# First chunk's blocks solved on VectorE and feed-forward groups of two chunks, in place of feed-forward groups of three chunks

## The chip, the cores and the metric

The kernel runs on one core of a Trainium2 chip. The core has five engines with queues of their own, each working through its instructions in order: TensorE (PE in the profile; its weight loads are shown apart as PEld), VectorE (DVE), ScalarE (ACT), GpSimd (POOL) and SyncE (SP, which only issues DMAs here). Engines wait for one another through semaphores. TensorE writes its results to PSUM, which DVE and ACT read; everything else is in SBUF, and the inputs, the output and some intermediate arrays are in HBM.

The metric is the device time of one execution in microseconds: 1093.16 us, the median of three runs (1090.8, 1093.16 and 1096.74). A difference of about 0.5% is the least that a measurement of this kernel can tell from none.

## What is computed

Two stages. The first is a recurrence over 768 positions for 4 batches of 8 heads, with a 40 x 40 state each; the second is a feed-forward layer with a squared ReLU over the 3072 tokens that come out. The weights of the second stage arrive as 64-bit floats, everything else as 32-bit floats.

```python
# r, k, v, w, a, b: (4, 8, 768, 40)
for t in range(S):
    y[:, :, t] = einsum('bhd,bhde->bhe', rt, state)
    Sa = einsum('bhde,bhe->bhd', state, at)
    state_decay = state * wt[:, :, None, :] - einsum('bhd,bhe->bhde', Sa, bt)
    state = state_decay + einsum('bhd,bhe->bhde', vt, kt)
x = y.transpose(0, 2, 1, 3).reshape(B * S, H * D)      # 3072 x 320
h = maximum(x @ w_in, 0.0)                              # 320 x 2048
out = h * h @ w_out                                     # 2048 x 320
```

## The kernel before

**Tiling.** The 768 positions are cut into chunks of 128. One unit of work is a chunk of one batch with all its 8 heads; there are 24, numbered so that chunk 0 to 3 are the first chunk of each batch, 4 to 7 the second, and so on. Only chunks of the same batch depend on each other through the state.

**Work of one chunk.** `early(i)` turns w, a and b with TensorE (line 316), multiplies the decays up along time (scans, lines 353 and 354; reciprocals, 357 and 358; products with b and a, 361 and 362), forms a matrix N of the chunk on TensorE, and stores N and the decays in HBM (`kept_q`, `kept_m`, `kept_n`, `kept_d`, `kept_e`). `solve(u)` inverts the triangular diagonal blocks of N: a loop of 31 or 63 steps, each of one multiplication (line 432, result in `half_p`) and one subtraction (line 434, in `half_t`), all on POOL. For the first chunks the blocks are 32 x 32 (31 steps), later 64 x 64. `take(u)` fetches a unit's blocks (`half_n`) before, and the result is stored to `kept_t`. `inverses(i)` fetches it as `blocks`, and puts the 64 x 64 inverse T together with a transposition on DVE (line 466) and small matmuls. `rest(i)` loads k, r, v and b of a chunk, turns them, and makes the masked products A and RV. `chain(i)` is the part that must go in the order of the chunks: x from A and the state, T, N, T again, a transposition, the new state (line 595), RX, and the chunk's output `tokens` (line 614).

**Feed-forward.** The generator `ffn()` takes the output of a group of `GB = 3` chunks at once: 384 columns. For each of 16 blocks of 128 hidden units it multiplies by `w_third` (64 rows: the remainder of the 320 input rows, two blocks side by side on the two halves of the array) and by `w_in` (two times 128 rows), then ACT applies ReLU (line 641) and DVE multiplies by the value before it, which squares it (line 642). Each 32-bit matmul shows as two in the profile. Two blocks make a pair, whose results lie in two PSUM buffers of the pool `ps_f`, which has two; the last group uses the pool `ps_w` with four. Then for each chunk of the group 16 matmuls by `w_out` (320 columns) are summed up. The generator yields after each block and after each quarter of a chunk's second part, so a group is 16 + 12 = 28 steps. Before a group can start, its `tokens` rows are moved to where the matmuls want them: eight small DMAs on SP.

**Weights.** Since they are 64-bit, `rounding()` makes 32-bit floats of them piece by piece with ACT and DVE (lines 258 to 277), 26 pieces in all, of which the first 10 are needed before feed-forward can start. The raw words are fetched into memory that is free at that time: `w_out` and the later `hid`.

**Order of the work.** It is written out by hand. A prologue calls the generators of chunks 0 to 3 step by step with `go`, with `solve(0)`, `solve(1)` and `solve(2)` in between. Then the loop over the 24 chunks interleaves ("weaves"), in 12 steps per chunk: `chain(i)`, `rest(i + 1)`, `early` of chunks further on, 10 steps of `ffn()` and some pieces of `rounding()`. In chunks 0 to 3 no feed-forward step runs, in chunk 4 there are 8 (from its step 4 on). What is left of `ffn()` runs after the loop. Each engine follows the order in which this program emits its instructions; a wait at the head of a queue stops all behind it. Loads and stores go through SP's queue in the order of emission, `take` and the store after `solve` through POOL's.

**Rings.** Inputs have ring buffers: two each for k, b and v, one for r.

Of the kernel before, what the change touches and what calls it, by code (L numbers as in the profile page):

```python
# [11 lines left out]
Alu = mybir.AluOpType  # L12
# [5 lines left out]
def kernel(  # L18
# [22 lines left out]
    nc = tc.nc  # L41
# [8 lines left out]
    NP = H // 2  # L50
    DP = 64
    NF = DFF // 128
    GB = 3

# [34 lines left out]
    def single(name, shape):  # L89
        return const.tile(shape, FP32, tag=name, name=name)  # L90
# [40 lines left out]

    def more_rings():
        for nm in ("k", "b", "r", "v"):
            rings[nm] = Ring(f"in_{nm}", 1 if nm == "r" else 2, [128, H, DP], 0.0, pads)

    order = [(bb, c) for c in range(NCH) for bb in range(B)]
    loaded, early_loaded = {}, {}
# [45 lines left out]

    UP, DOWN, A_ = range(3)
    decays = Ring("decay", 2, [128, 3, NP, C + 2], 1.0, whole)
    minus_x = Ring("minus_x", 1, [128, H, DP], 0.0, pads)
    states = Ring("state", B, [128, NP, 2, DP], 0.0, whole)

    w_in = single("w_in", [128, NT, DFF])
# [9 lines left out]


    room = w_out.rearrange("p f c -> p (f c)")
    hidden = single("hid", [128, NF, GB * C])
    free_words = hidden.rearrange("p f t -> p (f t)")
    lowest = single("lowest", [128, 1])
    nc.vector.memset(lowest, -896.0 * (1 << 23))
    wide = [room[:, 4 * WI * i:4 * WI * (i + 1)] for i in range(2)] + [free_words[:, :4 * WI]]

    in_turn = [free_words[:, at:at + 2 * DM] for at in [4 * WI + 2 * DM * i for i in range(4)] + [2 * DM * i for i in range(3)]]
    LENT = len(in_turn)


    runs = []
# [18 lines left out]
              [w_third[:, WI * i:WI * (i + 1)] for i in range(2)])  # L231
    NARROW = len(pieces)
    WIDE = len(fetches)
    for f in range(NF):
        fetchable(in_turn[f % LENT], [(0, 128, moe_w_out[f * 128:(f + 1) * 128, :])], [w_out[:, f, :]])

    then = {1: (3,), 2: (WIDE,), 3: (4,), 4: (WIDE + 1,), 5: (WIDE + 2,), 6: (WIDE + 3,), 7: (WIDE + 4,), 8: (WIDE + 5,),
            9: (WIDE + 6,)}
    then.update({NARROW + f: (WIDE + f + LENT,) for f in range(NF - LENT)})
    finished = [0]  # L240
    left = lambda: len(pieces) - finished[0]

# [93 lines left out]
    turned = lambda nm, bufs: new(nm, [128, NP, 128], bufs)  # L336


    def spare(name, i):
        at = NF * GB * C - (("mv", "turned", "joins").index(name) * 2 + i % 2 + 1) * H * Q  # L340
        return free_words[:, at:at + H * Q].rearrange("p (h t) -> p h t", h=H)

    def early(i, g=None):

# [63 lines left out]
        for col in range(cols):  # L408
            queues[col % len(queues)].dma_start(out=part_of(u)[col * rows:(col + 1) * rows], in_=kept)  # L409

    def solve(u, between={}):

        first, nb = units[u]
        fine = u < FINE
        size = Q if fine else HC
        cols = classes(u)
        rows = 128 // cols
        part = part_of(u)
        words = size // cols * size
        at = u * Q * Q // 2 if fine else 0  # L420
        ts = solved[:, at:at + words]
        nc.gpsimd.memset(ts, 0.0)
        for col in range(cols):
            nc.gpsimd.memset(ts[col * rows:(col + 1) * rows, col::size + cols], -1.0)
        t3 = ts.rearrange("p (j t) -> p j t", t=size)
        for s in range(size - 1):
            if s in between:
                between[s]()
            n, m_ = s // cols + 1, size - 1 - s
            at = s * size + s + 1 if s < Q else Q * HC + (s - Q) * (Q + 1) + 1  # L430
            p_ = new("half_p", [128, 528], 1)[:, :n * m_].rearrange("p (j t) -> p j t", j=n)
            nc.gpsimd.tensor_tensor(p_, part[:, at:at + m_].unsqueeze(1).to_broadcast([128, n, m_]),  # L432
                                    t3[:, :n, s:s + 1].to_broadcast([128, n, m_]), Alu.mult)
            nc.gpsimd.tensor_tensor(t3[:, :n, s + 1:], t3[:, :n, s + 1:], p_, Alu.subtract)  # L434
        to = kept_t[u]
        to = to.rearrange("n b h f k j t -> (n b h f k) (j t)") if fine else to.rearrange("n b h f j t -> (n b h f) (j t)")
        nc.gpsimd.dma_start(out=to, in_=ts)

# [52 lines left out]
    def rest(i, g):  # L491
# [14 lines left out]
        if soon(i):  # L506
            next(joining, None)
        yield
        g["A"] = masked("A", 2, kT, aT)
        yield  # L510
        while "v" not in x_:
            line.pop(0)[1]()
# [113 lines left out]
    def ffn():  # L626
        for gi in range(len(order) // GB):
            while gi not in gathered or finished[0] < NARROW:
                yield False
            t_ = tokens.pop(gi)  # L630
            hid = []
            for f in range(0, NF, 2):
                ps = [psum(ps_f if gi < len(order) // GB - 1 else ps_w)[:, :GB * C] for _ in range(2)]
                for e, p_ in enumerate(ps):
                    half = slice(e * DP, (e + 1) * DP)
                    mm(p_, w_third[half, f * 64:f * 64 + 128], t_[half, NT, :], True)
                for e, p_ in enumerate(ps):
                    for j in range(NT):
                        mm(p_, w_in[:, j, (f + e) * 128:(f + e + 1) * 128], t_[:, j, :], False)
                    h_ = hidden[:, f + e]  # L640
                    nc.scalar.activation(h_, p_, Act.Relu)  # L641
                    nc.vector.tensor_tensor(h_, p_, h_, Alu.mult)  # L642
                    hid.append(h_)
                    yield True
            while left():
                yield False
            for n in range(GB):
                bb, c = order[gi * GB + n]
                p_ = psum(ps_f if gi < len(order) // GB - 1 else ps_w)[:, :DM]
                for f in range(NF):  # L650
                    mm(p_, hid[f][:, n * C:(n + 1) * C], w_out[:, f], f == 0)
                    if f % PART == PART - 1 and f < NF - 1:
                        yield True
                o_ = new("o", [128, DM], 2)
# [6 lines left out]

    second = ffn()
    gathered = set()

    def run(gen):
        for _ in gen:
# [87 lines left out]
    tc.no_sync_barrier()  # L754


    TOTAL = 12
    ahead = {0: (4, 5), 1: (6, 7), 2: (8,), 3: (9,), 4: (10, 11), 5: (12, 13)}
    ahead.update({i: (i + 8,) for i in range(6, len(order) - 8)})
    share = {**{i: (0, 0) for i in range(B)}, B: (8, 4)}  # L760
    pieces_in = {0: (4, TOTAL), 1: (6, TOTAL), 2: (6, TOTAL), 3: (7, TOTAL), B: (4, 4)}
    done = set(range(B))
    unit = unit_of[B]
    for i in range(len(order)):
        bb, c = order[i]
# [10 lines left out]
        for j, m_ in enumerate(made):  # L776
            jobs.append((prepare(m_), 5, j * 5, TOTAL - 5 * (len(made) - 1 - j)))
        done.update(made)
        jobs.append((some(second, n), n, begin, TOTAL))
        if i in pieces_in:  # L780
            m_, end = pieces_in[i]
            jobs.append((some(rounded, 2 * m_), 2 * m_, 0, end))
# [38 lines left out]
```

## Time and profile before

| | before |
|---|---|
| median of three runs | 1093.16 us |
| profiled execution, whole time | 1096.74 us |
| profiled execution, span from first to last instruction | 1095.0 us |
| mean granted TensorE clock | 0.905 |
| HBM read and written | 75.77 and 34.48 MB |
| chunk outputs (line 614): first five | 92.8, 142.5, 189.3, 228.7, 274.4 us |
| chunk outputs: last | 1025.3 us |
| first feed-forward matmul | 244.8 us |
| POOL's last instruction in the table of stages | before 900 us |

The profile is of one execution. Its busy times count an engine's own instructions; the span is what they are shares of. Times in the timeline are counted from the span's start. The page's picture of the span in 40 slices shows TensorE at nine tenths or more from the eleventh slice (274 us) on, with a break in the last slices but two, and the granted clock between 0.5 and 0.8 of full speed in the first nine.

### The profile page before, as it was taken

What the parts mean: (1) busy time and instruction counts of PE and PEld (TensorE: products, weight loads), DVE (VectorE), ACT (ScalarE), POOL (GpSimd) and SP (SyncE); (2) the same over time, 40 slices, a digit from 0 to 9 for tenths busy, and PEclk for the clock granted to TensorE, in tenths of its full rate; (3) what the DMA queues carried; (4) which work ended last, traced back from release to release, by engine and by line L of the source; (5) the groups of instructions that cost most, each with busy time, mean ns of one, the idle gap of its engine ahead of it and who ended that gap; (6) DMA issues with size and microseconds to landing.
All of it is one profiled execution on the core that took longest, in us unless ns stands there. A gap on an engine that the chain in (4) does not pass through costs nothing.

```text
span 1095.0 us, 18413 instructions
## 1 busy us (share of the span) xinstructions
PE 996.7 (91%) x7248; PEld 746.5 (68%) x7248; DVE 470.3 (43%) x940; ACT 236.1 (22%) x483; POOL 653.2 (60%) x1127
## 2 busy tenths in 40 slices
PE   6286667889999999999999999999999999999798
PEld 5275566776677766777677667766786777667556
DVE  6458666686453265243452463252323322331030
ACT  2133222332221222113211222113112211230020
POOL 5787636885885999923999904999858820000000
PEclk8656655568999999899999999999999999999899
DMA  9879987767819524348616528414244331330000
GB/s 113 156 145 182 182 217 152 154 123 150 146 62 206 119 75 68 100 116 159 132 40 111 119 83 161 116 46 80 54 115 92 68 85 32 73 62 7 22 1 18
DMA packets 261350, 113.42 MB, mean 104 GB/s; under 512 B 243792, under 2 KB 249424, under 8 KB 259600
## 3 DMA queue, kind: packets, MB, share of 16 engines
q1 hardware_dynamic: 256928, 93.24, 43.3%
q0 software_dynamic: 3248, 18.88, 7.2%
q8 instruction: 57, 0.93, 0.4%
q10 hardware_dynamic: 1088, 0.13, 0.1%
q14 instruction: 29, 0.24, 0.1%
HBM read 75.77 MB, written 34.48 MB: 101 GB/s over the span
## 4 chain that ended last, share of the span: by engine, by line
PE 75%; DVE 9%; DMA 8%; POOL 3%; SPq 2%; issue 2%; ACT 1%; DVEq 0%; POOLq 0%; ACTq 0%
PE ps_f L87 35%; PE ps_c L87 19%; PE ps_w L87 13%; PE ps_w L316 4%; PE ps_w L532 1%; DMA half_n<-kept_d 1%; POOL half_p L432 1%; DMA dec<-kept_e 1%; DMA blocks<-kept_t 1%; POOL half_t L434 1%; SPq L108 1%; DVE decay L357 1%; DVE decay L358 1%; PE ps_c L542 1%; PE ps_c L585 1%
## 5 line engine op out<-in xcount | busy, mean ns | idle before, releaser
L432 POOL TENSOR_TENSOR half_p<-half_n,half_t 128x70 f32<-128x70 f32 (+52 forms) x502 | 289.4, 576 | 102.4 <-DMA half_n<-kept_d 53.8
L434 POOL TENSOR_TENSOR half_t<-half_t,half_p 128x70 f32<-128x70 f32 (+52 forms) x502 | 316.1, 630 | 39.3
L87 PE MATMUL ps_f<-w_out,hid 128*128 128x320 f32 x672 | 199.5, 442 | 0.0
L87 PE MATMUL ps_f<-tokens,w_in 128*128 128x384 f32 x448 | 174.6, 514 | 0.0
L642 DVE TENSOR_TENSOR hid<-ps_f,hid 128x384 f32<-128x384 f32 x112 | 61.8, 552 | 232.2 <-ACT hid L641 232.1
L87 PEld LDWEIGHTS ps_f<-w_out,hid 128*128 128x128 f32 x672 | 122.6, 192 | 44.4 <-issue 1.4
L87 PEld LDWEIGHTS ps_f<-tokens,w_in 128*128 128x128 f32 x448 | 78.0, 193 | 63.9 <-issue 33.2
L641 ACT ACTIVATE hid<-ps_f 128x384 f32<-128x384 f32 x112 | 55.0, 491 | 217.4 <-PE ps_f L87 217.4
L87 PEld LDWEIGHTS ps_c<-xr,T 64*64 64x64 f32 x768 | 55.4, 151 | 25.7 <-issue 22.1
L87 PE MATMUL ps_f<-tokens,w_third 64*128 64x384 f32 x224 | 62.2, 536 | 2.4 <-DVE w_out L266 1.3
L87 PE MATMUL ps_c<-xr,T 64*64 64x40 f32 x768 | 61.3, 242 | 3.3 <-ACT xr L566 1.0
L87 PEld LDWEIGHTS ps_c<-in_v,A 128*128 128x128 f32 x384 | 50.3, 206 | 4.1
L332 DVE TENSOR_TENSOR A<-ps_w,upper 128x512 f32<-128x512 f32 x48 | 30.9, 685 | 48.3 <-PE ps_w L87 48.3
L87 PE MATMUL ps_c<-in_v,A 128*128 128x40 f32 x384 | 49.6, 292 | 0.0
L332 DVE TENSOR_TENSOR RX<-ps_w,upper 128x512 f32<-128x512 f32 x48 | 30.8, 684 | 39.9 <-PE ps_w L87 39.8
L409 POOL DMA_DIRECT2D half_n<-kept_d x18 | 9.0, 504 | 64.7 <-DMA kept_d<-N 64.4
L353 DVE TENSOR_TENSOR_SCAN decay<-ps_w,ones 128x64 f32<-128x64 f32 x88 | 23.7, 270 | 51.2 <-PE ps_w L316 51.2
L87 PE MATMUL ps_w<-decay,bT 40*128 40x128 f32 x352 | 28.5, 308 | 17.9 <-DVE decay L362 15.6
L503 DVE TENSOR_TENSOR kvT<-ps_w,dec 128x512 f32<-128x512 f32 x24 | 16.4, 683 | 61.3 <-PE ps_w L316 36.6
L87 PE MATMUL ps_w<-rT,xnT 40*128 40x128 f32 x384 | 33.3, 302 | 9.7 <-DVE RV L332 8.6
L614 DVE TENSOR_TENSOR tokens<-ps_c,dec 128x512 f32<-128x512 f32 x24 | 16.5, 689 | 59.3 <-PE ps_c L87 59.3
L87 PEld LDWEIGHTS ps_w<-rT,xnT 40*128 40x128 f32 x384 | 27.8, 202 | 19.9 <-DVE RV L332 14.0
(138 smaller groups left out, 1456.6 us busy)
## 6 DMA issues: line engine op xcount, KB each, us to landing
kept_e<-decay SPq DMA_DIRECT2D x22, 780.0 KB
dec<-kept_e SPq DMA_DIRECT2D x22, 780.0 KB
hid<-in_moe_w_out_dram SPq DMA_DIRECT2D x16, 320.0 KB
half_n<-kept_d POOLq DMA_DIRECT2D x12, 384.0 KB, 10.2
half_n<-kept_d POOLq DMA_DIRECT2D x6, 768.0 KB, 11.0
in_w<-in_w_dram SPq DMA_DIRECT2D x24, 160.0 KB
in_ab<-in_b_dram SPq DMA_DIRECT2D x24, 160.0 KB
in_ab<-in_a_dram SPq DMA_DIRECT2D x24, 160.0 KB
```

Source lines behind the costliest of these rows:

```text
L87: nc.tensor.matmul(o, l_, r_, start=start, stop=True, skip_group_check=True)
L108: later(lambda: queue.dma_start(out=out_, in_=in_), steps)
L316: nc.tensor.transpose(p_[:, q * 128:(q + 1) * 128], pair(x_, q), ident)
L332: nc.vector.tensor_tensor(t_, p_, over4(upper), Alu.mult)
L353: nc.vector.tensor_tensor_scan(up[:, q, MID + 1:C + 1], wT[:, q, MID:], ones, 1.0, Alu.mult, Alu.mult)
L357: nc.vector.reciprocal(down[:, :, MID + 1:C + 1], up[:, :, MID + 1:C + 1])
L432: nc.gpsimd.tensor_tensor(p_, part[:, at:at + m_].unsqueeze(1).to_broadcast([128, n, m_]), t3[:, :n, s:s + 1].to_broadcast([128, n, m_]), ...
L434: nc.gpsimd.tensor_tensor(t3[:, :n, s + 1:], t3[:, :n, s + 1:], p_, Alu.subtract)
L503: nc.vector.tensor_tensor(kT, kT_, down[:, :, 1:C + 1], Alu.mult)
L614: nc.vector.tensor_tensor(t_, y_, g["up"][:, :, :C], Alu.mult)
L641: nc.scalar.activation(h_, p_, Act.Relu)
L642: nc.vector.tensor_tensor(h_, p_, h_, Alu.mult)
```

## The change

The feed-forward part works on groups of two chunks (256 columns) instead of three (384). With `GB = 2` there are 12 groups, a group has 16 + 8 = 24 steps, and 12 steps of it run in each chunk from chunk 4 on; in chunk 4, 8 more are emitted ahead of the chunk's other work. The hidden units get a 17th slot, and their slots go round. All weight pieces are made in chunks 0 to 3. With the memory that becomes free, two raw buffers of their own take weights, and the rings of r and of `minus_x` get a second buffer, A four buffers instead of two; the output buffer `o` has one instead of two.

In the prologue the first chunk's blocks are solved on DVE, with the intermediate product in PSUM, and stored and fetched through ACT's queue. Chunk 0's A, r and v steps and the loads of chunk 1 and of the third early chunk are emitted ahead of it, the decays of chunks 2 and 3 after it; the fetch of chunk 1's blocks follows it in the program but is on POOL's queue, which `solve(0)` no longer uses.

```diff
-    GB = 3
+    GB = 2
...
-            rings[nm] = Ring(f"in_{nm}", 1 if nm == "r" else 2, [128, H, DP], 0.0, pads)
+            rings[nm] = Ring(f"in_{nm}", 2, [128, H, DP], 0.0, pads)
...
-    minus_x = Ring("minus_x", 1, [128, H, DP], 0.0, pads)
+    minus_x = Ring("minus_x", 2, [128, H, DP], 0.0, pads)
...
-    hidden = single("hid", [128, NF, GB * C])
+    hidden = single("hid", [128, NF + 1, GB * C])
...
+    lent = [free_words[:, 2 * DM * i:2 * DM * (i + 1)] for i in range(3)]
+    own_ = [single(f"raw{i}", [128, 2 * DM]) for i in range(2)]
...
-    def solve(u, between={}):
+    def solve(u, between={}, engine=nc.gpsimd):
...
-            p_ = new("half_p", [128, 528], 1)[:, :n * m_].rearrange("p (j t) -> p j t", j=n)
-            nc.gpsimd.tensor_tensor(p_, part[:, at:at + m_].unsqueeze(1).to_broadcast([128, n, m_]),
+            p_ = new("half_p", [128, 528], 1) if engine is nc.gpsimd else psum(ps_f)
+            p_ = p_[:, :n * m_].rearrange("p (j t) -> p j t", j=n)
+            engine.tensor_tensor(p_, part[:, at:at + m_].unsqueeze(1).to_broadcast([128, n, m_]),
                                     t3[:, :n, s:s + 1].to_broadcast([128, n, m_]), Alu.mult)
-            nc.gpsimd.tensor_tensor(t3[:, :n, s + 1:], t3[:, :n, s + 1:], p_, Alu.subtract)
+            engine.tensor_tensor(t3[:, :n, s + 1:], t3[:, :n, s + 1:], p_, Alu.subtract)
...
-        nc.gpsimd.dma_start(out=to, in_=ts)
+        (nc.gpsimd if engine is nc.gpsimd else nc.scalar).dma_start(out=to, in_=ts)
...
-        g["A"] = masked("A", 2, kT, aT)
+        g["A"] = masked("A", 4, kT, aT)
...
-                    h_ = hidden[:, f + e]
+                    h_ = hidden[:, (gi * NF + f + e) % (NF + 1)]
...
-                o_ = new("o", [128, DM], 2)
+                o_ = new("o", [128, DM], 1)
...
+    STEPS = NF + 4 * GB
...
-    solve(0, {12: lambda: take(1, own)})
+    go(r0, 2)
+    load_early(3)
+    load(1)
+    flush()
+    solve(0, engine=nc.vector)
+    join = inverses(0, ready[0], nc.scalar)
+    go(join)
+    take(1, own)
     go(r0)
-    load_early(3)
-    go(r0, 4)
-    go(e2, 2)
-    load(1)
+    go(e2)
+    go(r0, 2)
     go(first_slot)
-    go(e2, 2)
-    go(e3, 2)
+    go(e2)
+    go(join)
+    go(e2)
+    go(e3)
+    go(join)
+    go(e2)
+    go(e3)
+    go(join)
...
-    join = inverses(0, ready[0])
-    go(join)
...
-    solve(1, {8: lambda: weights_by(0, nc.gpsimd), 20: lambda: take(2, own)})
+    solve(1, {14: lambda: weights_by(0, nc.gpsimd)})
+    take(2, own)
...
-    TOTAL = 12
+    TOTAL = STEPS // GB
...
-    share = {**{i: (0, 0) for i in range(B)}, B: (8, 4)}
-    pieces_in = {0: (4, TOTAL), 1: (6, TOTAL), 2: (6, TOTAL), 3: (7, TOTAL), B: (4, 4)}
+    share = {**{i: (0, 0) for i in range(B)}, B: (TOTAL, 8)}
+    pieces_in = {0: 4, 1: 7, 2: 8, 3: 8}
...
-        n, begin = share.get(i, (10, 0))
+        n, before = share.get(i, (TOTAL, 0))
+        for _ in range(before):
+            next(second)
+            tick()
...
-        jobs.append((some(second, n), n, begin, TOTAL))
+        jobs.append((some(second, n), n, 0, TOTAL))
```

More of the change, by code (lines that the diff above doesn't have):

```diff
@@ L206 @@
     wide = [room[:, 4 * WI * i:4 * WI * (i + 1)] for i in range(2)] + [free_words[:, :4 * WI]]
-    in_turn = [free_words[:, at:at + 2 * DM] for at in [4 * WI + 2 * DM * i for i in range(4)] + [2 * DM * i for i in range(3)]]
-    LENT = len(in_turn)
+    lent = [free_words[:, 2 * DM * i:2 * DM * (i + 1)] for i in range(3)]
+    own_ = [single(f"raw{i}", [128, 2 * DM]) for i in range(2)]
     runs = []
@@ L233 @@
     WIDE = len(fetches)
+    in_turn = [*own_, *lent]
     for f in range(NF):
[L235 to L239, printed above, removed]
+        fetchable(in_turn[f % 5], [(0, 128, moe_w_out[f * 128:(f + 1) * 128, :])], [w_out[:, f, :]])
+    then = {0: (WIDE,), 1: (3,), 2: (WIDE + 1,), 3: (4,), 5: (WIDE + 2, WIDE + 3), 6: (WIDE + 4,)}
+    then.update({NARROW + f: (WIDE + f + 5,) for f in range(NF - 5)})
     finished = [0]
@@ L339, in spare @@
     def spare(name, i):
-        at = NF * GB * C - (("mv", "turned", "joins").index(name) * 2 + i % 2 + 1) * H * Q
-        return free_words[:, at:at + H * Q].rearrange("p (h t) -> p h t", h=H)
+        n = ("mv", "turned", "joins").index(name)
+        t_ = hidden[:, NF - 2 * n - i % 2] if i <= B else own_[n // 2][:, n % 2 * H * Q:(n % 2 + 1) * H * Q]
+        return t_.rearrange("p (h t) -> p h t", h=H)
     def early(i, g=None):
@@ L778 @@
         done.update(made)
-        jobs.append((some(second, n), n, begin, TOTAL))
+        jobs.append((some(second, n), n, 0, TOTAL))
         if i in pieces_in:
-            m_, end = pieces_in[i]
-            jobs.append((some(rounded, 2 * m_), 2 * m_, 0, end))
+            jobs.append((some(rounded, 2 * pieces_in[i]), 2 * pieces_in[i], 0, TOTAL))
         weave(*jobs)
```

## The prediction

> **What bounds the kernel now.** I read the page first: busy times, the chain that ended last, and TensorE's clock.
>
> ```profile
> PE 996.7 (91%) x7248; PEld 746.5 (68%) x7248; DVE 470.3 (43%) x940; ACT 236.1 (22%) x483; POOL 653.2 (60%) x1127
> PE 75%; DVE 9%; DMA 8%; POOL 3%; SPq 2%; issue 2%; ACT 1%; DVEq 0%; POOLq 0%; ACTq 0%
> ```
>
> Three quarters of the closing chain are TensorE's. A share over the whole span hides stages, so next I cut the span at the writes of `tokens` (one per chunk; the first at 92.8, then 142.5, 189.3, 228.7 and 274.4 us) and asked for busy times by stage. Columns: the window, its length, busy time and count of PE, PEld, DVE, ACT, POOL, then granted clock, DMA share, GB/s.
>
> ```profile
> 59.00:93.00 34.00, 25.37 (x236) 23.00 (x236) 24.47 (x47) 10.64 (x21) 27.81 (x83) 0.70 0.87 153
> 93.00:142.00 49.00, 33.87 (x300) 30.87 (x300) 37.04 (x68) 14.12 (x27) 33.58 (x91) 0.63 0.96 191
> 142.00:189.00 47.00, 32.97 (x240) 29.65 (x240) 29.00 (x59) 12.98 (x28) 22.95 (x56) 0.54 0.78 175
> 189.00:229.00 40.00, 32.57 (x278) 28.95 (x276) 27.85 (x61) 12.14 (x27) 35.73 (x55) 0.60 0.63 145
> 229.00:274.00 45.00, 43.18 (x351) 33.01 (x350) 33.72 (x73) 15.25 (x33) 28.81 (x70) 0.77 0.80 142
> 274.00:1025.00 751.00, 737.39 (x5412) 540.58 (x5408) 280.32 (x557) 149.75 (x306) 464.36 (x635) 0.99 0.44 92
> ```
>
> So there are two regimes. From 274 us TensorE is busy 98% at a clock of 0.99: whatever adds TensorE time there adds it to the end. Before 229 us nothing is full, the clock is 0.54 to 0.70, and DMA and VectorE are busiest. Last, TensorE's own timeline at the end:
>
> ```profile
> 1025.14 2.42 PE L87 MATMUL ps_f<-w_out,hid 128*128 128x320 f32 x8
> 1032.41 2.98 PE L87 MATMUL ps_w<-tokens,w_third 64*128 64x384 f32 x4 [4.85 <-DMA tokens<-tokens]
> 1040.49 0.92 PE L87 MATMUL ps_w<-tokens,w_third 64*128 64x384 f32 x4
> ```
>
> The last group waits for its `tokens` transfers, and its first pair of blocks runs slowly (8.08 us to the next pair).
>
> **Part A: more joints between matmuls.** Two hidden blocks form a pair: 4 matmuls on `w_third` (two at a time, on different row halves) and 8 on `w_in`. A back-to-back pair, the release of its output buffers, and a pair with attention woven in:
>
> ```profile
> 1058.60 0.92 PE L87 MATMUL ps_w<-tokens,w_third 64*128 64x384 f32 x4
> 1059.45 2.85 PE L87 MATMUL ps_w<-tokens,w_in 128*128 128x384 f32 x8
> 1062.23 0.92 PE L87 MATMUL ps_w<-tokens,w_third 64*128 64x384 f32 x4
> 1058.71 0.49 ACT L641 ACTIVATE hid<-ps_w 128x384 f32<-128x384 f32 x1 [0.80 <-PE ps_w L87]
> 1059.23 0.56 DVE L642 TENSOR_TENSOR hid<-ps_w,hid 128x384 f32<-128x384 f32 x1 [0.73 <-ACT hid L641]
> 412.43 0.92 PE L87 MATMUL ps_f<-tokens,w_third 64*128 64x384 f32 x4
> 413.27 1.56 PE L87 MATMUL ps_f<-tokens,w_in 128*128 128x384 f32 x4
> 414.76 1.12 PE L87 MATMUL ps_c<-xr,T 64*64 64x40 f32 x16
> 416.31 1.46 PE L87 MATMUL ps_f<-tokens,w_in 128*128 128x384 f32 x4
> 417.69 1.12 PE L87 MATMUL ps_c<-minus_x,N 64*64 64x40 f32 x16
> ```
>
> The timeline's last row of matmuls is 96 of 320 columns in 26.00 us: 0.271 us each, 0.847 ns a column, loads hidden. For 384 columns that is 0.325 us, and a pair should take (8 + 2) x 0.325 = 3.25 us. It takes 1062.23 - 1058.60 = 3.63 back to back, and 2.33 + 1.38 = 3.71 woven. The surplus, 0.38 to 0.46, sits where the shape changes. Going from 384 to 256 columns leaves the number of columns as it is (3 x 256 = 2 x 384), but 8 groups of 8 pairs become 12 groups of 8: 32 pairs more. Low: 32 x 0.38 = 12 us. High: all rows of that layer on the page, (174.6 + 25.2 + 62.2 + 9.4) / 64 = 4.24 us a pair, so 32 x 0.99 = 32 us; but that mean holds slow-clock stretches and waits. I take 0.55, near the woven row: **+18 us**. The second layer keeps its 768 matmuls.
>
> The Trainium skill, "TensorE: Matmul & The Clock Gate", Part 3, section "The mechanism", speaks against the change: a weight load overlaps running matmuls only when the row group differs. With its load of 128 columns / 1.2 per ns (same page, section "LDWEIGHTS"), 256 more full-array loads would cost an estimated 27 us. The row with 0.271 us shows same-shape loads hidden; by the rule the sum would end 9 us higher.
>
> **Part B: two output buffers and fewer columns to hide behind.** Pool `ps_f` has two buffers, one per block of a pair. The next pair's second block needs ACT (L641) and then DVE (L642) to have finished the last one. From the rows: 1059.23 + 0.56 - 1058.60 = 1.19 us after the block's last matmul. With 128 columns fewer (ACT 491 against 426 ns for 384 and 320 columns, DVE 552 against 481): 1.19 - 0.13 - 0.14 = 0.92. In the changed kernel's instruction order, 18 places put a pair directly after a pair in `ps_f` (10 in the loop, 4 ahead of chunk 4, 4 after the last chunk); now every such place is in the four-buffered `ps_w`. Each stops TensorE; the other block's third-rows go first, so the loss is at most 0.92 + 0.65 (two passes alone) - 0.85 (both together) = 0.72. Low 0, high 13; I take 0.6: **+11 us**. Behind the wait is TensorE's whole queue, attention included.
>
> **Part C: the end.** After the last chunk 40 feed-forward steps remain, the first 16 of group 10. They cover the last gather. Gone: 1032.41 - 1027.4 = 5.0 us, and the slow pair, 8.08 - 3.63 = 4.45. **-9.5 us** (bounds -9.5 and -5, should the clock still fall).
>
> **Part D: 20 steps instead of 8 in chunk 4.** That stage has 1.8 us idle and a clock of 0.77. If the missing 0.23 is time at half clock, that is 45 x 0.46 = 21 us slow, worth at most 10. The early 8 steps meet the slow clock themselves. Bounds -12 and +3; I take **-5**.
>
> **Part E: the start.** The moved solve and what it replaces (columns as before):
>
> ```profile
> 22.96 0.24 POOL L432 TENSOR_TENSOR half_p<-half_n,half_t 128x31 f32<-128x31 f32 x1 [3.46 <-DMA half_n<-kept_q]
> 47.14 0.21 POOL L434 TENSOR_TENSOR half_t<-half_t,half_p 128x8 f32<-128x8 f32 x1
> 879.46 0.17 DVE L523 TENSOR_TENSOR f<-f,same 128x8 f32<-128x8 f32 x1
> 879.66 0.52 DVE L524 TENSOR_TENSOR state<-state,f 128x320 f32<-128x320 f32 x1
> ```
>
> On POOL it takes 47.35 - 22.96 = 24.4 us, 2.0 of them issuing chunk 1's transfers (31.59). On DVE: 62 dependent operations of 50 elements on average. Dependent small ones start 0.20 apart (879.46, 879.66); elements cost (0.52 - 0.17) / 312 = 1.1 ns, so 0.055; a PSUM result read next costs about 0.08 more (72.74 to 73.53 for an operation of 0.68). Per step 2 x 0.255 + 0.08 = 0.59; times 31, 18 us. Bounds: 62 x 0.20 = 12.4 and, by the longest start-to-start here (879.04 to 879.46), 26.
>
> The solve is 6 us shorter, but its cover goes. While POOL solved, DVE ran chunks 2 and 3's decays (26.81 to 38.62, 11.8 us) and then idled 15.6 us. Now these queue behind: 22.96 + 18 + 2.0 (masks, k, b) + 11.8 + 0.45 (transpose of the blocks) + some 2 waiting for the blocks' round trip (47.65 to 54.23 before, now through ACT's queue: one store, four loads) = 57.2; TensorE's products for chunk 3 (2.08) stand ahead of chunk 0's T: 59.3, against 59.20 before. **Nil.** Chunk 1's solve starts some 16 us earlier on POOL, but its blocks kept DVE only 1.2 us and ACT 3.0: -2. Four more weight pieces (27 against 23) before chunk 4, 5 x 0.48 us of DVE each, 9.6 us in stages where DVE is 62 to 76% busy: +3. SP's gather of the first group, 6.8 us for eight issues, now comes before chunk 3's loads, not chunk 4's: +2. The second r buffer: -1. Together **+2** (bounds -13 and +12).
>
> By the Trainium skill, "GPSIMD Engine Reference", section 3.1, an addition of two tensors runs 1.96 times faster on VectorE; an estimate for the solve is then 12.4 us, and the sum would end 5.6 us lower. No row here has the same shape on both engines.
>
> **Sum.** 18 + 11 - 9.5 - 5 + 2 = +16.5 on the profiled span of 1095.0. That execution took 1096.74, 1.7 around the span, 3.6 above the median of 1093.16. On the median: **1109.7 us**.
>
> **Rivals.** *Joints are cheap* (15%): ACT and DVE release in time and a joint costs 0.38: 16.5 - 11 - 6 = -0.5, 1092.7. For it: of all waits after 250 us only 1.1 us is for `hid`. Against: every pair there had other work or four buffers.
>
> *The start follows POOL* (12%), the other side: if chunks 1 to 4 wait for solved blocks, all 24.4 us removed from POOL's queue come off. 16.5 - 2 - 24.4 = -9.9, 1083.3; from 14.5 us of gain it is level, from 20 measurably faster. For it: POOL busy 27.81 of 34 in the window from 59. Against: the waits for blocks above, 4.2 us.
>
> *DVE bounds the start* (15%): the solve at 26 us and rounding queue in full: E becomes +12, 1119.7. For it: DVE is busy without a break from 85.87 to 98.7. Against: it then idles at 115 and 121 to 127.
>
> **How the numbers follow.** My forecast has 58%, with its own range 1101 to 1120 (B at 0 or A near its high end). The whole range, 1090 to 1122, reaches to the cheap joints and to the bound start, and leaves out the POOL case and the far ends. Measurement tells 0.5% (5.5 us) from no change. Faster: the POOL case 10, cheap joints 3: 13%. Within 0.5%: cheap joints 10, my low edge 3, POOL 2: 15%. Slower: 72%.
>
> **What would show it.** A: pairs of 256 columns near 0.55 + 10 x 0.217 = 2.7 us. B: TensorE waits on `hid` (L644) at the 18 places. C: no gap before the last group, clock 1.0 there. D: chunk 4's stage at a higher clock. E: the first T of chunk 0 at 59 to 60 us, the fourth `tokens` near 231. I am wrong if that one comes before 215, or if pairs cost 2.4 us.

## The result and the profile after

The changed kernel takes 1143.15 us (median of four runs, 1140.93 to 1150.66) where the kernel before, beside it, takes 1093.77: a ratio of 1.046 with a 95% interval of 1.041 to 1.052. The forecast was 1109.7, with a range that ended at 1122: the direction held, the loss is three times as large. The profiled execution has a span of 1139.2 us against 1095.0, so 44.2 us are to be found. A few executions further below took over 1.5% longer than the fastest of their kernel; the medians and ratios leave them out.

The page of the changed kernel, busy times and chain of waits:

```profile
PE 1032.9 (91%) x7632; PEld 814.2 (71%) x7632; DVE 491.9 (43%) x1066; ACT 246.3 (22%) x547; POOL 636.0 (56%) x1066
PE 69%; DVE 12%; DMA 12%; SPq 3%; ACT 2%; issue 2%; POOL 0%; ACTq 0%; DVEq 0%; POOLq 0%
```

TensorE has 384 instructions more (32 pairs of 12) and is 36 us longer busy; but its share of the closing chain falls from 75 to 69%, while those of VectorE (9 to 12%), DMA (8 to 12%) and SP's queue (2 to 3%) grow. So more waits have come into the chain as well. The stages of the changed kernel, cut at its own writes of `tokens` (columns as before: window, length, PE, PEld, DVE, ACT, POOL, granted clock, DMA share, GB/s):

```profile
191.00:231.00 40.00, 32.25 (x282) 28.70 (x278) 32.32 (x70) 14.03 (x31) 35.76 (x55) 0.62 0.59 137
231.00:288.00 57.00, 54.91 (x434) 42.06 (x432) 28.78 (x63) 14.77 (x35) 41.21 (x92) 0.94 0.60 115
288.00:1062.00 774.00, 745.28 (x5629) 580.96 (x5626) 281.85 (x601) 154.88 (x349) 454.42 (x617) 0.98 0.42 90
1062.00:1098.00 36.00, 34.68 (x128) 22.75 (x128) 5.34 (x12) 4.65 (x12) 0.00 (x0) 1.00 0.03 10
1098.00:1139.00 41.00, 38.00 (x162) 26.07 (x160) 6.80 (x16) 7.43 (x19) 0.00 (x0) 1.00 0.04 13
```

The start ends 2.5 us later (231.2 against 228.7). Chunk 4's stage is 57 us for 45.7, but has 12 feed-forward steps more in it, at a clock of 0.94 for 0.77. The loop from chunk 5 to 23 takes 774 for 751, though it now does 19 x 12 = 228 of 288 feed-forward steps (19 chunks' worth) where it did 190 of 224 (20.4): by the feed-forward columns in the two traces it should have been 21 us shorter. In this window the loss lies. Last, TensorE's waits there, with the total, the number and the longest of each, first in the changed kernel and then in the kernel before:

```profile
PE ps_w L87 <- DVE RV L331: 6.1, 6, 1.7
PE ps_w L87 <- DVE kvT L505: 5.8, 1, 5.8
PE ps_w L534 <- DVE RX L331: 5.7, 10, 0.7
PE ps_f L87 <- DVE hid L644: 3.9, 13, 0.7
...
PE ps_w L532 <- DVE RX L332: 6.6, 10, 0.8
PE ps_w L87 <- DVE RV L332: 3.8, 3, 1.9
PE ps_f L87 <- DVE hid L642: 1.1, 3, 0.5
```

Three of the first four are waits of the attention (the first stage's matrices), not of the feed-forward part. The one of 5.8 us, for `kvT`, is new.

The steps that the prediction named, in the changed kernel's timeline (start, length, engine, line; in brackets the idle time ahead and who ended it):

```profile
22.92 0.20 DVE L434 TENSOR_TENSOR ps_f<-half_n,half_t 128x31 f32<-128x31 f32 x1 [2.24 <-issue]
...
58.05 1.92 PE L87 MATMUL ps_c<-xr,T 64*64 64x40 f32 x16
...
231.23 0.69 DVE L616 TENSOR_TENSOR tokens<-ps_c,dec 128x512 f32<-128x512 f32 x1 [3.03 <-PE ps_c L87]
...
1064.55 1.99 PE L87 MATMUL ps_f<-tokens,w_in 128*128 128x256 f32 x8
1066.58 0.38 ACT L643 ACTIVATE hid<-ps_f 128x256 f32<-128x256 f32 x1 [0.48 <-PE ps_f L87]
1066.62 0.70 PE L87 MATMUL ps_f<-tokens,w_third 64*128 64x256 f32 x2
1067.00 0.42 DVE L644 TENSOR_TENSOR hid<-ps_f,hid 128x256 f32<-128x256 f32 x1 [0.44 <-ACT hid L643]
1067.48 0.70 PE L87 MATMUL ps_f<-tokens,w_third 64*128 64x256 f32 x2 [0.17 <-DVE hid L644]
1068.10 1.99 PE L87 MATMUL ps_f<-tokens,w_in 128*128 128x256 f32 x8
...
1098.25 0.70 PE L87 MATMUL ps_w<-tokens,w_third 64*128 64x256 f32 x4
1098.88 1.99 PE L87 MATMUL ps_w<-tokens,w_in 128*128 128x256 f32 x8
1100.81 0.70 PE L87 MATMUL ps_w<-tokens,w_third 64*128 64x256 f32 x4
```

At the start, chunk 0's T is used at 58.05 (before: 59.20). At the end, a pair in the two-buffered `ps_f` takes 1068.10 - 1064.55 = 3.55 us: the second block's matmuls on `w_third` are split off and wait for VectorE's product to free the buffer. In the four-buffered `ps_w` the same pair takes 1100.81 - 1098.25 = 2.56, with the four matmuls together.

### The profile page after: what moved, and what is told of

It is laid out like the page before. It is cut to its first block, busy times and chain, and to the rows that moved or that the text cites. A ratio compares the mean times of both kernels' runs of the same rounds, so it can differ in the third digit from the quotient of the medians.

```text
span 1139.2 us, 19328 instructions
## 1 busy us (share of the span) xinstructions
PE 1032.9 (91%) x7632; PEld 814.2 (71%) x7632; DVE 491.9 (43%) x1066; ACT 246.3 (22%) x547; POOL 636.0 (56%) x1066
## 4 chain that ended last, share of the span: by engine, by line
PE 69%; DVE 12%; DMA 12%; SPq 3%; ACT 2%; issue 2%; POOL 0%; ACTq 0%; DVEq 0%; POOLq 0%
PE ps_f L87 33%; PE ps_c L87 19%; PE ps_w L87 11%; PE ps_w L315 3%; DMA in_v<-in_v_dram 2%; SPq L108 2%; DMA in_w<-in_w_dram 2%; DVE decay L358 2%; DVE decay L359 2%; PE ps_w L534 1%; DMA dec<-kept_e 1%; DVE RV L331 1%; DVE RX L331 1%; DMA in_b<-in_b_dram 1%; DVE hid L644 1%
## 5 line engine op out<-in xcount | busy, mean ns | idle before, releaser
L434 POOL TENSOR_TENSOR half_p<-half_n,half_t 128x252 f32<-128x252 f32 (+47 forms) x471 | 281.9, 599 | 117.2 <-DMA half_n<-kept_d 54.7
L436 POOL TENSOR_TENSOR half_t<-half_t,half_p 128x252 f32<-128x252 f32 (+47 forms) x471 | 306.7, 651 | 36.9
L644 DVE TENSOR_TENSOR hid<-ps_f,hid 128x256 f32<-128x256 f32 x176 | 74.0, 421 | 345.3 <-ACT hid L643 344.9
L87 PE MATMUL ps_f<-tokens,w_in 128*128 128x256 f32 x704 | 198.0, 408 | 0.0
L87 PEld LDWEIGHTS ps_f<-tokens,w_in 128*128 128x128 f32 x704 | 123.8, 194 | 43.2 <-issue 30.3
L643 ACT ACTIVATE hid<-ps_f 128x256 f32<-128x256 f32 x176 | 67.6, 384 | 272.3 <-PE ps_f L87 271.8
L87 PE MATMUL ps_f<-tokens,w_third 64*128 64x256 f32 x352 | 86.3, 425 | 7.6 <-DVE hid L644 5.7
L87 PEld LDWEIGHTS ps_f<-tokens,w_third 64*128 64x128 f32 x352 | 40.1, 190 | 34.5 <-DVE hid L644 22.9
L354 DVE TENSOR_TENSOR_SCAN decay<-ps_w,ones 128x64 f32<-128x64 f32 x88 | 23.8, 270 | 82.7 <-PE ps_w L315 82.7
L87 PE MATMUL ps_w<-rT,xnT 40*128 40x128 f32 x384 | 36.7, 311 | 11.6 <-DVE RV L331 10.9
L315 PE MATMUL ps_w<-ident,in_ab 128*128 128x128 f32 x192 | 34.3, 335 | 12.6 <-DVE RV L331 10.4
L546 ACT COPY sd<-ps_c 128x512 f32<-128x512 f32 x20 | 11.7, 586 | 146.2 <-PE ps_c L544 146.1
L87 PE MATMUL ps_w<-decay,bT 40*128 40x128 f32 x352 | 29.7, 316 | 11.1 <-DVE decay L363 10.2
```

Source lines behind the costliest of these rows:

```text
L87: nc.tensor.matmul(o, l_, r_, start=start, stop=True, skip_group_check=True)
L315: nc.tensor.transpose(p_[:, q * 128:(q + 1) * 128], pair(x_, q), ident)
L354: nc.vector.tensor_tensor_scan(up[:, q, MID + 1:C + 1], wT[:, q, MID:], ones, 1.0, Alu.mult, Alu.mult)
L434: engine.tensor_tensor(p_, part[:, at:at + m_].unsqueeze(1).to_broadcast([128, n, m_]), t3[:, :n, s:s + 1].to_broadcast([128, n, m_]), Alu ...
L436: engine.tensor_tensor(t3[:, :n, s + 1:], t3[:, :n, s + 1:], p_, Alu.subtract)
```

## The experiments

All times are medians; each ratio is against the kernel before, run beside it, with its 95% interval. Traces are of one execution each. The changed kernel itself was run once more, beside some of the later experiments:

> The changed kernel itself, as the base on this chip for the runs beside it: 1143, within 1138-1150.

1144.31 us, ratio 1.048 (1.046 to 1.050). The profiled span is 1141.2.

**The gathers on SP's queue.** The wait of 5.8 us for `kvT` is VectorE's for the transfer of `dec` (6.7 us, until 535.1). SP's queue of the changed kernel ahead of it:

```profile
509.49 6.26 SPq L108 DMA_DIRECT2D tokens<-tokens  x8
515.85 1.39 SPq L450 DMA_DIRECT2D T<-kept_t  x2
...
521.10 0.56 SPq L142 DMA_DIRECT2D in_k<-in_k_dram  x1
521.72 0.63 SPq L152 DMA_DIRECT2D dec<-kept_e  x1
522.39 0.43 SPq L142 DMA_DIRECT2D in_r<-in_r_dram  x1
522.87 5.53 SPq L142 DMA_DIRECT2D in_v<-in_v_dram  x1
```

Eight gathers take 6.3 us of the queue, and T, N, k and `dec` stand behind them. `dec` is issued at 521.72, 0.2 us ahead of POOL's fetch of a unit's blocks (2 x 768 KB), and arrives some 13 us later:

```profile
521.93 0.52 POOL L410 DMA_DIRECT2D half_n<-kept_d  x1 [42.47 <-DMA kept_d<-N]
```

The edit moves the gathers back:

```diff
-                store(t_[row:row + m_, j], t_[at:at + m_, h // 2], 1)
-            later(lambda: gathered.add(i // GB), 2)
+                store(t_[row:row + m_, j], t_[at:at + m_, h // 2], 4)
+            later(lambda: gathered.add(i // GB), 5)
```

> The changed kernel, with the eight gathers of a group's tokens issued on SP's queue three steps later, behind the next chunk's loads (k, dec, r, v, b) instead of ahead of them. Theory (the gathers come every second chunk now and hold the loads back by 6 us; the wait for dec of 5.8 us and the slow clock after it come from that): 6 to 12 us less, 1131-1137. Rival (the loads have slack except in one chunk, and the gathers are then late themselves): 0 to +3.

1126.86 us, ratio 1.032 (1.028 to 1.035): 16 us less. Its queue at the same place, and POOL's fetch:

```profile
506.56 1.94 SPq L450 DMA_DIRECT2D T<-kept_t  x2
508.56 0.71 SPq L459 DMA_DIRECT2D N<-kept_n  x1
509.44 6.33 SPq L108 DMA_DIRECT2D tokens<-tokens  x8
...
518.67 0.61 SPq L142 DMA_DIRECT2D in_k<-in_k_dram  x1
519.33 0.64 SPq L152 DMA_DIRECT2D dec<-kept_e  x1
...
520.33 1.03 POOL L410 DMA_DIRECT2D half_n<-kept_d  x2 [39.93 <-DMA kept_d<-N]
```

T goes out 9 us earlier and `dec` 2.4; there is no wait for `dec` left, and that chunk takes 40.1 us for 50.4. (Here the gathers still stand ahead of k, since all that is queued is issued when a unit's blocks are fetched; where no unit is fetched, k, `dec` and r go first.) The place of the gathers in the queue counts, and for more than the theory said. How it counts is less plain. In the two traces the spans differ by 9.8 us (1139.2 and 1129.4), and chunk 10 alone gains 10.2; in the others gains and losses cancel (chunk 11 loses 4.2, chunks 14 and 18 gain 4.1). So in these traces the gathers do not cost 6.3 us each time, but nearly all in one place.

At this place the gathers stand ahead of `dec` in both kernels. What differs is that `dec` goes out 1.0 us ahead of POOL's fetch and not 0.2. In sixteen traces (all but that of the first early release below), seven have `dec` 0.2 to 0.3 us ahead here, and TensorE waits 1.9 to 6.5 us for it (chunk 10 takes 42.2 to 52.2 us); nine have it 0.6 to 1.0 us ahead, and the wait is 0.8 us at most (38.6 to 41.9). That the two transfers get into each other's way fits this, but no run moved the fetch alone; and with the square on ACT, below, one wait of 6.4 us for `dec` in chunk 6 came with a lead of 0.8.

The same edit on the kernel before:

> The kernel before with the gathers behind the loads alone. Theory (of the 8 us that both edits gave there, the start of the loop gave most: three steps of the chunks with rounding came earlier by 2 to 3.5 us each): -4 to -8, 1085-1089. Rival (the early release gave it): 1090-1093.

1088.20 us, ratio 0.996 (0.995 to 0.998): 4 us less. There, a gather comes every third chunk. So some 12 of the 16 us belong to the change, by medians.

**What follows a wait in the clock.** Around the wait for `dec` in the changed kernel, by windows (columns as above):

```profile
529.80:535.40 5.60, 0.27 (x3) 0.03 (x1) 0.29 (x1) 0.84 (x2) 0.00 (x0) 1.00 1.03 180
535.40:542.20 6.80, 6.34 (x32) 5.33 (x33) 2.52 (x6) 0.39 (x1) 4.55 (x12) 0.50 1.47 137
542.20:549.00 6.80, 6.80 (x54) 5.63 (x53) 5.60 (x10) 1.46 (x3) 6.09 (x10) 1.00 0.27 43
```

TensorE stands idle for 5.6 us, and the next 6.8 us are granted at half speed (the half clock, 0.50 in the second row): with them the stretch costs 5.6 + 3.4 us. In the loop the changed kernel spends 34.1 us at half clock in eight stretches, the kernel before 13.7 in three: 10 us of the loss. With the gathers moved it is still 30.7, so most of the half clock does not come from them.

**The start.** The solve alone put back on POOL:

```diff
-    solve(0, engine=nc.vector)
-    join = inverses(0, ready[0], nc.scalar)
+    solve(0)
+    join = inverses(0, ready[0])
```

> The changed kernel with the first chunk's blocks solved on POOL again (24.4 us there, 15.4 on VectorE), its round trip on the queues of before, all else in the new order. Theory (chunk 0's result waits for the solve, and the new order has no cover left): the first tokens 6 to 9 us later, and the whole 5 to 9 us longer, 1148-1152. Rival (the start is bound by DMA and VectorE's other work): within 3 us of 1143. Rival (VectorE was the bound there): 3 to 6 us shorter.

1147.79 us, ratio 1.051 (1.048 to 1.055): 4 to 5 us longer, at the edge of what the theory said. In its trace T is used at 64.72 (6.7 us later) and the fourth `tokens` come at 242.8 (11.6 later); chunk 10 then takes 41.9 us instead of 50.4, without a wait for `dec`, which gives part of it back. So with the new order the start does follow the solve. The other way round, the kernel before with the new start (and one `o` buffer, for room):

> The kernel before with the start of the changed one alone: chunk 0's solve on VectorE, its round trip on ACT's queue, the inputs of chunks 1 and 3 ahead, two r buffers; one o buffer to make room. Groups of three chunks as before. Theory (the start is worth +2.5 us, as the fourth tokens say): fourth tokens at 229-233, the whole 1093-1098. Rival (the shorter solve does help, and the changed kernel's start is held by its four more weight pieces): fourth tokens before 222, 1083-1088.

1097.01 us, ratio 1.004 (1.003 to 1.006); fourth `tokens` at 232.1. So the faster solve (15.4 us on VectorE, 22.92 to 38.33, for 24.4 on POOL) and the order around it give together 3 to 6 us of loss. Part E had this portion at -3: its +3 for four more weight pieces and +2 for the earlier gather are not in this kernel.

**The buffers.** The first try lets two successive pairs share the two banks, each a half:

```diff
-                ps = [psum(ps_f if gi < len(order) // GB - 1 else ps_w)[:, :GB * C] for _ in range(2)]
+                side = f // 2 % 2
+                if side == 0:
+                    banks = [psum(ps_f if gi < len(order) // GB - 1 else ps_w) for _ in range(2)]
+                ps = [p_[:, side * GB * C:(side + 1) * GB * C] for p_ in banks]
```

> The changed kernel, but two successive pairs of hidden blocks share the two banks of ps_f (256 columns each half), so that four blocks are in flight where two were; order of instructions unchanged. Theory (the release of the output buffers was under-sized: a pure pair takes 3.6 us in ps_f and 2.58 in ps_w): the 18 direct places give back about 1.0 us each, and the pairs with attention between them some 0.1 to 0.2 each: 1143 to 1115-1125. Rival (the surplus is the joints between shapes): only the 8 pure places ahead of chunk 4 and after the last chunk move, -8: 1135. Rival (the clock: stalls there bring the slow clock): -18 and also fewer slow stretches, below 1115.

1144.47 us, ratio 1.048 (1.045 to 1.051): nothing. Its trace says why: after the last chunk a pair still takes 3.55 us, and its second block still waits for VectorE. So no more blocks were in flight than before (whether the chip or the program's own waits between the halves of a bank are the reason is open), and the experiment tells nothing about the theory. On top of it, fewer changes of shape (`ps` here holds four blocks, two to a bank):

```diff
-            for f in range(0, NF, 2):
+            for f in range(0, NF, 4):
...
-                for e, p_ in enumerate(ps):
-                    half = slice(e * DP, (e + 1) * DP)
-                    mm(p_, w_third[half, f * 64:f * 64 + 128], t_[half, NT, :], True)
+                for n, p_ in enumerate(ps):
+                    half = slice(n % 2 * DP, (n % 2 + 1) * DP)
+                    at = (f + n // 2 * 2) * 64
+                    mm(p_, w_third[half, at:at + 128], t_[half, NT, :], n < 2)
```

> The same half banks, and the matmuls on w_third of two pairs issued together ahead of the w_in matmuls of both: 48 changes between the two shapes where there are 96; the same number of columns. Theory (each change of shape costs 0.3 to 0.5 us): 15 to 24 us below the kernel with half banks alone. Rival (the surplus is waits, not shapes): within 5 us of the kernel with half banks alone.

1137.24 us, ratio 1.041 (1.038 to 1.044): 7 us below the half banks, between both theories. By the two pages the matmuls on `w_third` are busy 73.7 us for 94.5, those on `w_in` 215.0 for 214.7, while TensorE's idle time from the fourth `tokens` on grows from 31 to 40 us. The 21 us hold both fewer changes of shape and fewer waits for a buffer, since a pair of pairs stops only once; so the 0.3 to 0.5 for each change is not shown.

A real second pair of buffers, for the last but one group (condition `gi < len(order) // GB - 2`):

> The changed kernel, with the last but one group's outputs in the four-buffered ps_w, as the last group's are. Four pure pairs after the last chunk should then take 2.58 us and not 3.55: theory (two buffers stop a pure pair) -4 us on the end, no wait on hid after the last chunk; 1136-1142. Rival (the first half of that group, woven with attention, now takes buffers away from it): 1143-1147.

1136.47 us, ratio 1.040 (1.037 to 1.042); 71.9 us from the last `tokens` to the end of the span instead of 77.3. Its timeline there:

```profile
1064.95 0.70 PE L87 MATMUL ps_w<-tokens,w_third 64*128 64x256 f32 x4
1065.58 1.99 PE L87 MATMUL ps_w<-tokens,w_in 128*128 128x256 f32 x8
1067.51 0.70 PE L87 MATMUL ps_w<-tokens,w_third 64*128 64x256 f32 x4
```

2.56 us a pair: two buffers were what stopped it. The end gives 5.4 us of the 7 to 8 that the whole got shorter; in this trace chunk 10 also takes 42.7 us instead of 50.4, which varies between kernels as said above. Next, an earlier release everywhere: the square is taken from ACT's copy, and the PSUM buffer is free after ACT.

```diff
-                    nc.vector.tensor_tensor(h_, p_, h_, Alu.mult)
+                    nc.vector.tensor_tensor(h_, h_, h_, Alu.mult)
```

> The changed kernel; the square of the hidden block is taken from ACT's copy in SBUF (hid * hid) and no longer from the PSUM buffer (PSUM * hid), so that a buffer of ps_f is free after ACT's 0.39 us and not after VectorE's 0.42 us behind it. The result is the same; order and number of instructions too. Theory (release of the two buffers: 18 pairs directly on a pair lose 1.0 us, 8 pairs behind 0.53 us of attention lose 0.2 and 10 lose 0.56): 18 x 0.5 + 8 x 0.2 + 10 x 0.5 = 16 us less, 1125-1130, and TensorE waits on hid no more than half as long. Rival (the wait is hidden anyway, the time is the joints'): within 4 us of 1143.

1153.04 us (median of three), ratio 1.054 (1.049 to 1.060), slower than without. Once more, with the changed kernel beside it:

> The changed kernel with the early release, once more, since its first profile had a granted clock of 0.75 for long stretches. Theory (release counts by itself): 1128-1137, 7 to 15 below the changed kernel beside it. Rival (as long as the gathers stand ahead of the loads, what the release gives is lost to later waits): within 4 us of the changed kernel or above it, and the profile shows a longer wait for dec or for the loads.

1148.15 us, ratio 1.053 (1.049 to 1.056), against 1.048 for the changed kernel beside it. TensorE's waits in its loop, and VectorE and POOL at one place:

```profile
PE ps_w L87 <- DVE RV L331: 15.5, 8, 3.5
PE ps_w L87 <- DVE kvT L505: 6.5, 1, 6.5
PE ps_c L87 <- DMA T<-kept_t: 5.5, 3, 2.2
```

```profile
410.88 0.80 DVE L644 TENSOR_TENSOR hid<-hid 128x256 f32<-128x256 f32 x1
411.61 1.04 DVE L523 TENSOR_TENSOR f<-end,ends 128x4 f32<-128x4 f32 x1
412.69 0.17 DVE L524 COPY f<-f 128x4 f32<-128x4 f32 x1
412.89 1.04 DVE L525 TENSOR_TENSOR f<-f,same 128x8 f32<-128x8 f32 x1
...
410.16 1.25 POOL L436 TENSOR_TENSOR half_t<-half_t,half_p 128x504 f32<-128x504 f32 x1
411.49 1.15 POOL L434 TENSOR_TENSOR half_p<-half_n,half_t 128x525 f32<-128x525 f32 x1
412.71 1.20 POOL L436 TENSOR_TENSOR half_t<-half_t,half_p 128x525 f32<-128x525 f32 x1
```

The time is the rival's, though the wait that grew is not one for the loads. No wait for `hid` on VectorE is left, but RV's grew from 6.1 to 15.5. The reason stands in the second view: VectorE's operations with two operands in SBUF (L644 now, L523 and L525 as ever) end with POOL's running one, or up to 0.3 us after it: 0.80 us for the square, 1.04 for one of four elements. Of 149 squares between 288 and 1075 us, 39 took over 0.6 us here; with one operand in PSUM, as in the changed kernel, none of 156 took over 0.43. The Trainium skill, "SBUF — State Buffer", section "SBUF: two separate sides", has the rule: the port pair that VectorE and GpSimd share is an exclusive lock, and an operation of VectorE with two SBUF inputs needs it, against one of GpSimd that reads SBUF. These rows agree. So this edit mixed two effects. The half clock grew too: 68.3 us of the loop, where the changed kernel beside it has 37.5. With the gathers moved back as well:

> The changed kernel with the early release and with the gathers behind the loads. Theory (two separate causes, SP's queue 16 us and the buffers' release 16 us): they add, 1108-1114. Rival (both shorten the same stalls of the attention): 1120-1127.

1117.5 us (median of three), ratio 1.024 (1.021 to 1.027): 8 to 9 us below the gathers alone, between the two theories. Both on the kernel before:

> The kernel before with the same two edits. Theory (at 384 columns a pair covers the release, and a gather comes every third chunk, so little is lost there): 0 to -6, 1087-1093. Rival (the gathers hold the loads back there as well): -8 or more.

1084.48 us, ratio 0.992 (0.990 to 0.994): 8 us less, the rival's size; 4 of them are the gathers', as shown above, so the release counts at 384 columns too. The mixture is taken apart by a square on ACT; all 192 of its squares took 0.42 us, POOL's work or not:

```diff
-                    nc.vector.tensor_tensor(h_, p_, h_, Alu.mult)
+                    nc.scalar.activation(h_, h_, Act.Square)
```

> The changed kernel; the square is taken on ACT (Square of hid) behind the Relu, VectorE has no part in it any more. The buffer is free after the Relu as in the early release, but no VectorE instruction has both operands in SBUF beside POOL's work. Theory (the release is worth 7 to 15 us, and the early release lost it because 39 of its 149 squares took 0.7 to 1.4 us and not 0.42 while POOL worked, which held back RV): 1128-1138. Rival (a stall moved is a stall kept, whatever does the square): 1141-1150, with RV or dec waited for longer.

1131.70 us, ratio 1.036 (1.033 to 1.039): 11 to 13 us less, as the theory said. Not all of what the release gave arrived: between the traces TensorE's waits ahead of attention matmuls grow from 24 to 33 us after the fourth `tokens`. The time from a pair's first matmul on `w_third` to its first on `w_in`, taken from the matmul starts after the start-up, outside stretches at half clock (mean us, number of pairs):

| kernel | `ps_f`, directly behind feed-forward work | `ps_f`, behind attention | `ps_w` |
|---|---|---|---|
| before (384 columns) | none | 1.043 (55) | 0.846 (7) |
| before, square on ACT, gathers late | 1.489 (1) | 0.834 (53) | 1.009 (8) |
| changed (256 columns) | 1.539 (19) | 0.789 (65) | 0.633 (8) |
| changed, square on ACT | 1.174 (19) | 0.630 (64) | 0.633 (8) |

The 1.009 holds one wait for the last gather. With no wait it is 0.63 at 256 columns. So release costs the changed kernel 19 x (1.539 - 0.633) + 65 x (0.789 - 0.630) = 17.2 + 10.3 = 27.5 us. The kernel before pays for it too, 55 x (1.043 - 0.834) = 11.5. By this account the change's own part is 16. The times do not show that part: the same square takes 14 us off the kernel before with late gathers (1088.20 to 1074.16, below) and 11 to 13 off the changed one.

**All together.**

> The changed kernel with the square on ACT, the gathers behind the loads and the last but one group in ps_w. Theory (three separate costs): 1143 - 16 - 5 - 12 = 1110, within 1104-1115; what is left against the kernel before, some 18, is then the 32 more pairs' joints less what the end and chunk 4 gave. Rival (they overlap): 1116-1125.

1111.97 us (median of four), ratio 1.018 (1.014 to 1.021), near the sum (1110) and not the overlap. Still slower than the kernel before. And the kernel before with the square on ACT and the gathers behind the loads:

> The kernel before with the square on ACT and the gathers behind the loads. Theory (of the 8 us that the early release and the gathers gave there, 4 are the gathers'; VectorE loses 0.55 us for each of 128 blocks and has 43% of its time busy): 1078-1086. Rival (ACT's chain of copies for the attention is now held up by the squares): 1088-1095.

```profile
span 1074.7 us, 18376 instructions
PE 984.8 (92%) x7248; PEld 739.7 (69%) x7248; DVE 404.4 (38%) x812; ACT 301.1 (28%) x611; POOL 651.4 (61%) x1127
```

1074.16 us, ratio 0.984 (0.982 to 0.986): faster than both kernels. TensorE is busy 92% of a span that is 20 us shorter; its loop has 10.2 us of half clock (13.7 in the kernel before). Against this kernel, the changed one with the same edits, and the end's buffers besides, is 37 to 38 us longer, where without edits the medians are 49 apart. So what repairs the change also helps what it replaced, and three quarters of the loss are left. In its trace the first layer's matmuls, at full clock and without waits, still take 22 us more than in the trace of this kernel (30 before the edits), and the start 5; the rest is not assigned, since the changed kernel's trace is of an execution 12 us above its median.

## Why the prediction was wrong

Each term, beside what the two profiles show (span, us):

| term | forecast | measured | how |
|---|---|---|---|
| A, joints of 32 more pairs | +18 | +17 | 32 x 0.53: a woven pair with no wait takes 0.41 + 0.11 over its columns (medians of the runs of matmuls) |
| B, two output buffers | +11 | +16 | the table above, from traces; the times do not show it as the change's own |
| C, the end | -9.5 | -9.3 | 4.85 waited for the gather, and the slow pair, 8.08 - 3.63 = 4.45, both gone |
| D, chunk 4 | -5 | -6.7 | attention matmuls 30.5 to 24.8 us, loss to half clock in feed-forward matmuls 3.8 to 2.8 |
| E, the start | +2 | +2.5 | fourth `tokens` 228.7 to 231.2 |
| half clock in the loop | none | +10 | 13.7 to 34.1 us at half speed |
| attention's waits in the loop | none | +12 | idle times of TensorE over 0.4 us: 12.2 to 23.8 |

They make 41.5 of the 44.2 us; 2.7 are not assigned. A, C, D and the two last rows are readings of the two traces; the experiments bear on B, E and the gathers.

**A** was right: a pair back to back takes 2.56 us (2.7 was said), and the woven surplus of 0.53 is the 0.55 that was taken. That it is the change of shape, and not something else in the same place, rests on the step lengths (0.31 to 0.32 us from start to start at a change, 0.216 between equal matmuls); the experiment with fewer changes could not set it apart from the waits for buffers.

**B** had the right mechanism and places; the size was off. The step that failed is "0.92 + 0.65 (two passes alone) - 0.85 (both together) = 0.72". The release measured 0.94 and the lone passes 0.62, near what was said (the 0.65 was of 384 columns too, and fitted by luck); but the 0.85 was read from a pair of 384 columns, and at 256 the four matmuls together take 0.63. A direct place loses 0.9, not 0.6. The clause "now every such place is in the four-buffered `ps_w`" also missed that 55 woven pairs of the kernel before wait 0.2 us each; the woven pairs of the changed kernel wait about as much in all, so that this cancelled.

**C and D** came as said. **E** came as said in its sum: T at 58.05 where 59 to 60 was named, the fourth `tokens` at 231.2 where 231 was named. In its parts this was luck: the solve took 15.4 us where 18 was taken, and the kernel before with the new start has its fourth `tokens` at 232.1 without the weight pieces and the earlier gather that were to cost 5. The rival in which the start follows POOL falls, though the new order would be 11.6 us later at the fourth `tokens` with the solve on POOL: the gain is real and the reordering spends it.

**What is missing** is above all the last two rows, 22 us. The step that failed stands in part E: "SP's gather of the first group, 6.8 us for eight issues, now comes before chunk 3's loads, not chunk 4's: +2". The issues were counted for one group and at the start only. A group of two gathers every second chunk, twelve times for eight, and 6.3 us of issues stand ahead of the loads of the next chunk in SP's queue. Moving them back gave 16 us by medians in the changed kernel and 4 in the kernel before, so the term was worth some 12 and not 2; in the traces nearly all of it is the wait for `dec` in chunk 10 and the half clock after it, 9 of the 22 us. The second omission is the clock: 0.99 in the loop was taken as a state that stays. In the changed kernel's loop the six idle stretches of 1.0 us and more, 13.3 us in all, were each followed by half clock, 27.2 us in all: they were paid about twice over. What brings the waits other than that for `dec`, and the half clock after them, is not shown. That part of the attention's waits which stays after the gathers are moved (RV's, 7.3 us) is seen, and was not tried alone; that shorter feed-forward steps give VectorE's part of the attention less cover is a guess.

None of the rivals came. Their mistake was common: all four cases argued over TensorE's matmuls and the start, and the one line on a queue that only issues counted it once.

## What to carry to other kernels

When a change makes something periodic more frequent, count all that the period issues: not only the matmuls, but the transfers in an in-order queue, and what stands behind them each time. A size that shortens the work also shortens what hides a hand-over; take every term of such a bound from rows of the same size. An edit that frees a buffer earlier should not move an operand to where another engine holds the port. And try each repair on the old kernel too: here it kept most of its lead.

## What was not expected of the hardware

**Half clock follows short idle stretches.** In sixteen traces (all but that of the first early release), after 290 us and at full clock, TensorE was idle for 1.0 us or more 91 times; 75 times 3.4 us or more of half clock followed within 5.5 us. Of the 16 without, eight were below 1.2 us; the longest was 2.2. Half clock also came behind idle times of under 1 us (552.4 us in the changed kernel, behind 0.58 us), so the length alone does not decide. The Trainium skill, "TensorE: Matmul & The Clock Gate", section "Why this matters for your kernels", asks for no idle gap above about 3 us, which would leave all but 15 of the 91 free of cost; here, between 1.2 and 3 us, 53 of 61 were followed by half clock, and the measurement decides.

**VectorE waits for POOL's whole operation**, as shown above: 1.04 us for four elements, and up to 1.4 for a square of 0.42; of the squares, only those with both operands in SBUF.
